# Attention and a mixture of experts in one kernel: the last two attention pairs in turn, and the late routing in two chains

## The chip, the cores and the metric

The kernel runs on one core of a Trainium2 chip. The metric is the time of one execution in microseconds (us) of device time. The core has five engines with a queue each: PE (matrix products; PEld is its weight load), DVE (vector), ACT (scalar), POOL, and SP, which here only issues DMAs. Each engine takes its instructions in the order in which the program lists them; semaphores make one engine wait for another.

## What is computed

Queries, pooled in pairs of rows, attend to keys; the result is the input of a mixture of eight experts with the two best per token.

```python
B, H, S, D = q.shape                      # 4, 8, 1152, 64
q_pool = q.reshape(B, H, S // 2, 2, D).mean(axis=3)
scores = scale * np.matmul(q_pool, k.transpose(0, 1, 3, 2))
attn = softmax(scores)                    # minus the row's maximum, over the sum
x = np.matmul(attn, v)                    # -> (2304, 512): 4 x 576 tokens, 8 heads x 64
noisy = x @ w_gate + np.log1p(np.exp(x @ w_noise)) * noise
top2, top2_w = the two best of 8 experts, softmax over the two
for e in range(8):                        # w1: 512 x 1024, w2: 1024 x 512
    out[mask] += top2_w * (np.maximum(x[mask] @ w1[e], 0) @ w2[e])
```

## The kernel before

**Attention.** A pair is one head of two batches: sixteen pairs, i = 0 to 15, eight (one per head) for the first half of the tokens and eight for the second. A pair has nine chunks of 128 queries; three chunks are a segment, so there are 48 segments, n = 0 to 47, and segment n belongs to pair n // 3 and query group g = n % 3. Numbers are split into a high and a low 16-bit part, so that each product is made of several. Ahead of a pair's segments stands its preparation: loads (load_k, load_q, load_v: kr, qr, vr), high and low parts (kn, qn, vv), DMA transpositions (kt, qt), a copy of the keys (kt2), the maximum of the scores of each query (products on PE, L297, and reductions on DVE), and the transposition of the maxima with the queries' low part (qt2). A segment is worked in nine steps of 128 keys; two steps make a unit u, 216 units in all. Of a unit, PE makes the scores (L342, L343), ACT the exponential pf (L350), DVE or POOL the low part pl (L354), and PE, some four units later, the products with the values (L370, P x V below). When a segment is through, it is evacuated (L381 to L390) into xa (first half) or xr (second half), one tile per query group.

**The planner.** The attention phase and what is laid among it is not issued in the order of the code. Plan collects operations, each with its engine, an estimated cost, a key (its due time, in steps of 128 keys), the operations that it depends on and the buffers that it takes and gives back, and then issues, engine by engine, the one with the lowest key of those that can start within 0.25 us of the earliest. So keys, costs and dependences set the order on every engine; once issued, an engine's order is fixed. Keys of a pair's preparation are counted from b = 27 * i.

**Routing.** Route.steps(j, gs, ...) routes the query groups gs of half j: three DMA transpositions per group (xTg, L661), 36 small products (L671), a chain of small DVE instructions (tiles rt and ru, L675 to L789), in it a product that ranks the tokens (the rank product, L757 and L759), and at its end six scatters per group, which POOL issues as indirect DMAs and which write the tokens into each expert's list xg in DRAM (L99). The first half is one chain of three groups, laid among attention by the planner with a pace between the keys of its steps. The second half is three chains, one per group, each of which starts when that group's segments of all eight pairs are evacuated. They are soft: what is not issued when attention is through goes on as a generator between the blocks of the early experts (Moe.early).

**Experts.** The first 256 rows of the lists of experts 0 and 1 come from the first half alone. Route.early loads them by DMA transpositions (xe, and the tokens' meta rows, mte); its operations become ready 20 us after the last scatter of the first half has been issued. Moe.early works experts 0 and 1 on them: eight blocks f of products (L927, mm1), each with a high part hh on ACT and a low part hl on DVE (L936, L937), and two blocks of 24 products (L948, mm2), while the next weights are split (wh on ACT, wl on DVE, L872 and L874). Then Moe.run loads the remaining rows (xT, L882), which needs every scatter, and works all eight experts in full; that is the full expert stage.

## Time and profile before

| | us |
|---|---|
| median of the three runs shown | 912.49 |
| lowest and highest of them | 906.23, 916.42 |
| span of the profiled execution | 910.5 |
| PE busy | 830.6 (91%) |
| DVE busy | 532.0 (58%) |
| ACT busy | 446.5 (49%) |
| POOL busy | 369.0 (41%) |
| chain that ended last: PE, DVE, DMA | 69%, 15%, 6% |

The span goes from the first to the last instruction of one execution taken by the profiler. Busy shares are means over stages with different limits, so a stage has to be looked at by itself. PEclk is the matrix engine's granted clock as a share of full speed. In a timeline a row is the start, the duration, the engine, the line and what is written from what; the brackets at its end say how long the engine stood idle before it, and what released it. A pipelined product's duration overlaps the next one's.

### The profile page before, as it was taken

To read this page: it belongs to the slowest core of one execution; us is meant where nothing else is said; L and a number is where in the kernel's file an instruction comes from. 1 tells how busy PE (TensorE), PEld (TensorE's weight loads), DVE (VectorE), ACT (ScalarE), POOL (GpSimd) and SP (SyncE) were. 2 spreads that over 40 slices of the span, in tenths; PEclk is the share of its full clock that TensorE was granted. 3 is DMA by queue.
4 is the path that set the end of the run, shared out by engine and by line. 5 is a ranking of instruction groups with operands and counts; after the bars stand their busy time and mean duration, and the time that the engine had idled before them with its cause. 6 is when DMAs were issued, how large, how long until landed. Compare 5 with 4: busy or idle time off the path is not lost.

```text
span 910.5 us, 21013 instructions
## 1 busy us (share of the span) xinstructions
PE 830.6 (91%) x8686; PEld 542.0 (60%) x8686; DVE 532.0 (58%) x1248; ACT 446.5 (49%) x663; POOL 369.0 (41%) x326
## 2 busy tenths in 40 slices
PE   3799899999999788899968899999999999999995
PEld 0367666667677666677754455657465565746542
DVE  4988887988897798898858233343324241431200
ACT  4678787777776556677523223333333232322310
POOL 4347577666765576777204611010211203020132
PEclk9889999999999899999988999999999999999998
DMA  8898976898697935475486956363736437281133
GB/s 192 198 242 165 209 208 177 178 215 191 142 225 163 201 94 127 125 206 170 106 131 224 298 71 163 71 183 97 205 74 169 110 111 184 77 208 24 24 49 46
DMA packets 213636, 137.79 MB, mean 151 GB/s; under 512 B 150304, under 2 KB 183584, under 8 KB 213536
## 3 DMA queue, kind: packets, MB, share of 16 engines
q1 hardware_dynamic: 204896, 116.33, 52.6%
q0 software_dynamic: 8640, 20.08, 10.7%
q8 instruction: 69, 1.13, 0.5%
q14 instruction: 31, 0.25, 0.1%
HBM read 62.14 MB, written 35.44 MB: 107 GB/s over the span
## 4 chain that ended last, share of the span: by engine, by line
PE 69%; DVE 15%; DMA 6%; issue 5%; ACT 2%; POOL 2%; SPq 1%; POOLq 0%; ACTq 0%; DVEq 0%
PE pss L927 21%; PE psm L948 20%; PE psm L370 11%; PE psm L297 6%; PE pss L342 5%; PE pss L343 5%; DVE pl L354 3%; DVE rd L311 2%; DMA vr<-in_v_dram 1%; POOL xg L99 1%; DVE vv L281 1%; DVE mx L320 1%; PE psm L927 1%; DMA kr<-in_k_dram 1%; ACT pf L350 1%
## 5 line engine op out<-in xcount | busy, mean ns | idle before, releaser
L354 POOL TENSOR_TENSOR pl<-pf 128x768 f16<-128x768 f32 x149 | 236.1, 1596 | 133.0 <-ACT pf L350 124.0
L350 ACT ACTIVATE pf<-pss 128x768 f32<-128x768 f32 x216 | 174.2, 811 | 75.6 <-PE pss L343 70.0
L99 POOL DMA_INDIRECT out_dram<-y,mti x40 | 62.6, 1565 | 323.4 <-ACT y L953 318.1
L370 PEld LDWEIGHTS <-pf 128*128 128x128 bf16 (+1 forms) x2880 | 156.2, 101 | 61.7 <-issue 21.5
L370 PE MATMUL psm<-vv,pf 128*128 128x65 f16 (+2 forms) x2880 | 189.0, 199 | 2.3 <-DVE vv L281 0.9
L370 PE MATMUL psm<-vv,pl 128*128 128x65 f16 (+1 forms) x1440 | 176.5, 194 | 0.2 <-DVE pl L354 0.2
L342 PE MATMUL pss<-qt,kt 128*128 128x384 f16 (+1 forms) x576 | 150.8, 290 | 1.8 <-ACT pf L350 1.6
L343 PE MATMUL pss<-qt,kt 66*128 66x384 f16 (+1 forms) x576 | 151.3, 291 | 0.0
L937 DVE SCALAR_TENSOR_TENSOR hl<-pss,hh 128x640 f16<-128x640 f32 (+2 forms) x68 | 50.2, 738 | 156.8 <-ACT hh L936 156.8
L370 PEld LDWEIGHTS <-pl 128*128 128x128 f16 (+1 forms) x1440 | 127.5, 103 | 1.3 <-issue 1.0
L948 PE MATMUL psm<-wh,hh 128*128 128x512 f16 x320 | 122.7, 383 | 3.6 <-issue 3.6
L948 PE MATMUL psm<-wl,hh 128*128 128x512 f16 x320 | 122.7, 383 | 0.0
L948 PE MATMUL psm<-wh,hl 128*128 128x512 f16 x320 | 122.3, 382 | 0.0
L948 PEld LDWEIGHTS <-hh 128*128 128x128 f16 x640 | 62.8, 98 | 79.0 <-issue 6.2
L311 DVE CUSTOM_DVE_ANT_0 rd<-psm,rd 128x512 f32<-128x512 f32 x144 | 97.1, 683 | 19.8 <-ACT rd L305 19.2
L936 ACT ACTIVATE hh<-pss 128x640 f16<-128x640 f32 (+2 forms) x68 | 43.2, 635 | 131.5 <-PE pss L927 131.4
L953 ACT ACTIVATE y<-psm,mg 128x512 f32<-128x512 f32 x40 | 27.5, 689 | 152.5 <-issue 77.3
L305 ACT ACTIVATE rd<-psm 128x512 f32<-128x512 f32 x144 | 85.7, 596 | 27.2 <-PE psm L297 17.3
L297 PE MATMUL psm<-kt,qt 128*128 128x512 f16 (+3 forms) x320 | 78.8, 323 | 20.9 <-ACT rd L305 10.0
L927 PE MATMUL pss<-xT,fh 128*128 128x320 f16 (+1 forms) x448 | 83.5, 303 | 1.1 <-DMA xT<-xg 1.1
L927 PE MATMUL pss<-xT,wh 128*128 128x320 f16 (+1 forms) x448 | 83.5, 303 | 0.0
L297 PE MATMUL psm<-kd,qt 128*128 128x512 f16 (+1 forms) x160 | 59.0, 412 | 26.6 <-DVE mx L311 14.6
(157 smaller groups left out, 1196.2 us busy)
## 6 DMA issues: line engine op xcount, KB each, us to landing
xg<-zt SPq DMA_DIRECT2D x40, 260.0 KB
kr<-in_k_dram SPq DMA_DIRECT2D x32, 288.0 KB
vr<-in_v_dram SPq DMA_DIRECT2D x16, 576.0 KB
kr<-in_moe_w_dram SPq DMA_DIRECT2D x17, 512.0 KB
qr<-in_moe_w_dram SPq DMA_DIRECT2D x16, 512.0 KB
kn<-in_moe_w_dram SPq DMA_DIRECT2D x16, 512.0 KB
qr<-in_q_dram SPq DMA_DIRECT2D x31, 256.0 KB
vr<-in_moe_w_dram SPq DMA_DIRECT2D x15, 512.0 KB
```

What stands on the lines that cost most here:

```text
L99: i = nc.gpsimd.indirect_dma_start(out=out, out_offset=bass.IndirectOffsetOnAxis(ap=idx, axis=0), in_=src, in_offset=None, **kw)
L297: s.nc.tensor.matmul(ps[r, o:o + m.shape[1] * P], s.G.buf["qt", i][:, c, r], m, start=True, stop=True)
L305: s.nc.scalar.activation(s.G.buf["rd", i, c], s.G.buf["D", i, c], AF.Relu)
L311: s.nc.vector.tensor_tensor_reduce(out=rd, in0=s.G.buf["S", i, c], in1=rd, scale=1.0, scalar=-3.0e38, op0=ALU.add, op1=ALU.max, accum_out= ...
L342: mm(ps[:, a, o:o + w], kt[:, hh * NK + kc, :], qf[:, q0:q0 + w], start=True, stop=False)
L343: mm(ps[:, a, o:o + w], kt2[0:66, hh * NK + kc, :], qf2[0:66, q0:q0 + w], start=False, stop=True)
L350: s.nc.scalar.activation(s.parts(u)[0], s.G.buf["ps", u][:, :, 0:SG], AF.Exp, scale=0.125 / (IN_SCALE * IN_SCALE))
L354: (s.nc.vector if eng == "DVE" else s.nc.gpsimd).tensor_sub(pl, pf, ph)
L370: mm(ps[o:o + m, ci, 0:w], src[:, t % 2, ci * P + o:ci * P + o + m], vv[:, hh * NK + kc, a:b], start=st, stop=last and src is pl, skip_gro ...
L927: nc.tensor.matmul(ps[:, i, 0:N], w[:, dc, f * P:(f + 1) * P], xT[:, 2 * dc + x, i * N:(i + 1) * N], start=(n == 0), stop=(n == 11))
L937: s.nc.vector.scalar_tensor_tensor(hl, ps, 0.0, hh, op0=ALU.max, op1=ALU.subtract)
L948: nc.tensor.matmul(ps, h[:, f, b * P:(b + 1) * P], w[:, f, :], start=(n == 0), stop=(n == 23))
```

## The change

Four things are changed.

The order of the last six segments: a table SEQ says which pair and group segment n belongs to. Up to pair 13 it is as before; pairs 14 and 15 take turns, (14, 0), (15, 0), (14, 1), (15, 1), (14, 2), (15, 2). The preparation of pairs from 10 on gets earlier keys, three less for each pair, and the last evacuation gets an earlier one.

The late routing: groups 0 and 1 of the second half are one chain (its tiles are of six chunks instead of three), whose second group's transpositions depend on that group's own evacuations (more); group 2 is a second chain. Their operations on other engines than DVE have keys lower by 12.

The first half's routing: its first key is 245 instead of 250, its pace 0.8 instead of 1.2, its scatters follow each other at 2.5 us instead of 3.0, and the early expert loads become ready 10 us after it instead of 20.

In Moe.early the meta instructions of an early expert come behind its eight blocks.

```diff
+SEQ = [(i, g) for i in range(NPAIR - 2) for g in range(3)] + [(i, g) for g in range(3) for i in (NPAIR - 2, NPAIR - 1)]
             n, kc = divmod(2 * u + a, NK)
-            i, g = divmod(n, 3)
+            i, g = SEQ[n]
...
-            b = 27 * i
+            b = 27 * i - 3 * max(0, i - 9)
...
-                           lat=3.0, take=[("qt2", ("qt2", i))] if g == 0 or not x else (), give=[("qn2", i)], after=ready[0][0] if x and g else None)
-                    for y in ((m,) if x else (m - 2, m - 1, m)):
-                        ready[y] = [t] + [kc[h] for h in ((0,), (0, 1), (1,))[y % 3]]
+                           lat=3.0, take=[("qt2", ("qt2", i))] if g == 0 or not x else (), give=[("qn2", i)], after=ready[0, 0][0] if x and g else None)
+                    for y in ((g,) if x else (0, 1, 2)):
+                        ready[i, y] = [t] + [kc[h] for h in ((0,), (0, 1), (1,))[y]]
+            b = 9 * SEQ.index((i, 0))
...
-            pr = sorted({n // 3 for n in segs})
-            sc = op("PE", 0.66, 2 * u, lambda u=u: s.score(u), deps=[d for n in segs for d in ready[n]], take=[("wide", ("ps", u))],
+            pr = sorted({SEQ[n][0] for n in segs})
+            sc = op("PE", 0.66, 2 * u, lambda u=u: s.score(u), deps=[d for n in segs for d in ready[SEQ[n]]], take=[("wide", ("ps", u))],
                     give=[(x, i) for i in pr for x in ("kt", "kt2", "qt", "qt2")])
...
-            i = n // 3
+            i, g = SEQ[n]
...
-            k1 = 9 * n + 17
+            k1 = 9 * n + (17 if n < NSEG - 1 else 7)
-            s.ev[n] = op("DVE", 0.3, k1 + 1, lambda n=n: s.evac(n, 2), deps=[hi], give=[("pv", n)])
+            s.ev[i, g] = op("DVE", 0.3, k1 + 1, lambda n=n: s.evac(n, 2), deps=[hi], give=[("pv", n)])
...
         def then():
             for e in range(NEARLY):
-                op("SP", 2.6, 400 + 4 * e, lambda e=e: R.early(e), ready=G.now + 20.0)
-        s.route(R.steps(0, (0, 1, 2), s.sm, 14, 6, 0.8), 250, [s.ev[n] for n in range(24)], 3.0, then=then, pace=1.2)
-        for g in range(3):
-            s.route(R.steps(1, (g,), R.rp, 36, 15, 0.3), 450 + 9 * g, [s.ev[24 + 3 * i + g] for i in range(NH)], 0.7, True)
-
-    def route(s, gen, key, deps, slack, soft=False, then=None, pace=0.0):
+                op("SP", 2.6, 400 + 4 * e, lambda e=e: R.early(e), ready=G.now + 10.0)
+        s.route(R.steps(0, (0, 1, 2), s.sm, 14, 6, 0.8), 245, [s.ev[i, g] for i in range(NH) for g in range(3)], 3.0, then=then, pace=0.8)
+        late = [[s.ev[i, g] for i in range(NH, NPAIR)] for g in range(3)]
+        s.route(R.steps(1, (0, 1), R.rp, 14, 6, 0.3), 432, late[0], 0.7, True, more=late[1])
+        s.route(R.steps(1, (2,), R.rp, 18, 8, 0.3), 450, late[2], 0.7, True)
...
+    def route(s, gen, key, deps, slack, soft=False, then=None, pace=0.0, more=()):
...
-            G.op(eng, cost, due[0], lambda: piece(bank, held), deps=deps, gen=gen if soft else None, **kw)
+            G.op(eng, cost, due[0] - (12 if soft and eng != "DVE" else 0), lambda: piece(bank, held), deps=deps, gen=gen if soft else None, **kw)
...
             wait, eng, cost = d if isinstance(d, tuple) else (0.0, "DVE", 0.3)
+            nxt = more if eng == "SP" and wait == 0.0 else ()
...
             else:
-                add(eng, cost, ready=ready)
+                add(eng, cost, ready=ready, deps=nxt)
...
-                yield (3.0 if j == 0 else 0.3, "POOL", 1.3) if gap else None
+                yield (2.5 if j == 0 else 0.3, "POOL", 1.3) if gap else None
...
                 yield 1.28
-                if f == 0:
-                    s.meta(e, 0, EARLY)
                 s.flush(KEEP)
                 for c in SPL[f]:
                     s.split(e, "2", c)
             s.flush()
+            s.meta(e, 0, EARLY)
```

The other two uses of divmod(n, 3), in pv and evac, are replaced like the first.

What this does to the order on the engines, in three places. The first is on SP, in the middle of the first half's routing (its groups' transpositions are xTg from xa). Before, the value load of pair 11 (vr) came behind the kt2 copies and a qt2 transposition:

```order
L661 DMA_TRANSPOSE xTg_5063<-xa2_133 128x8x128
L661 DMA_TRANSPOSE xTg_5085<-xa2_133 128x8x128
L661 DMA_TRANSPOSE xTg_5104<-xa2_133 128x8x128
L428 DMA kt2_0_121<-kt_0_94 64x1152 x2
L287 DMA_TRANSPOSE qt2_1_106<-qn2_1_127 128x9x128
L277 DMA vr_72<-in_v_dram 128x2x576
```

Now it stands ahead of them, with one clearing of the output between it and the transpositions:

```order
L665 DMA_TRANSPOSE xTg_4947<-xa2_133 128x8x128
L665 DMA_TRANSPOSE xTg_4968<-xa2_133 128x8x128
L665 DMA_TRANSPOSE xTg_4991<-xa2_133 128x8x128
L520 DMA out_0_dram<-zt_130 128x2x256
L278 DMA vr_72<-in_v_dram 128x2x576
L288 DMA_TRANSPOSE qt2_1_106<-qn2_1_127 128x9x128
L429 DMA kt2_0_121<-kt_0_94 64x1152
```

The second place is on SP at the end of attention. xr0 to xr2 are the second half's groups, L803 and L806 (now L807 and L810) loads of the first expert's weights, qt2_1_106 is the buffer of pair 15's maxima. Before, from pair 14's values on:

```order
L277 DMA vr_72<-in_v_dram 128x2x576 x2
L287 DMA_TRANSPOSE qt2_1_106<-qn2_1_127 128x9x128
L803 DMA kr_70<-in_moe_w1_dram 128x1024
L806 DMA qr_71<-in_moe_w2_dram 128x2x512
L806 DMA kn_73<-in_moe_w2_dram 128x2x512
L806 DMA vr_72<-in_moe_w2_dram 128x2x512
L806 DMA kr_70<-in_moe_w2_dram 128x2x512
L661 DMA_TRANSPOSE xTg_7818<-xr0_83 128x8x128
L661 DMA_TRANSPOSE xTg_7850<-xr0_83 128x8x128
L661 DMA_TRANSPOSE xTg_7882<-xr0_83 128x8x128
L661 DMA_TRANSPOSE xTg_7951<-xr1_84 128x8x128
L630 DMA_TRANSPOSE xe0_7971<-xg_82 128x8x256
```

Now, from the same load on (L288 is L287 of before, L634 and L636 are L630 and L632, L665 is L661):

```order
L278 DMA vr_72<-in_v_dram 128x2x576
L634 DMA_TRANSPOSE xe0_7058<-xg_82 128x8x256
L636 DMA mte0_7060<-xg_82 128x2x16
L634 DMA_TRANSPOSE xe1_7120<-xg_82 128x8x256
L636 DMA mte1_7122<-xg_82 128x2x16
L288 DMA_TRANSPOSE qt2_1_106<-qn2_1_127 128x9x128
L278 DMA vr_72<-in_v_dram 128x2x576
L807 DMA kr_70<-in_moe_w1_dram 128x1024
L810 DMA qr_71<-in_moe_w2_dram 128x2x512
L810 DMA vr_72<-in_moe_w2_dram 128x2x512
L810 DMA kn_73<-in_moe_w2_dram 128x2x512
L665 DMA_TRANSPOSE xTg_7587<-xr0_83 128x8x128
```

The early expert loads xe0 and xe1 with their meta rows moved from behind the late groups' first transpositions to ahead of pair 15's qt2; pair 15's values come behind that.

The third place is on PE in the first early expert. Before, the first rank product (tri and ones, for group 0 of the second half alone) stood six products into mm2:

```order
L948 LDWEIGHTS hl_8060
L948 MATMUL psm1_66<-wh2_8088,hl_8060 128x512
L757 LDWEIGHTS tri_353
L757 MATMUL psm2_67<-ru3_8362,tri_353 128x32
L759 LDWEIGHTS ones_355
L759 MATMUL psm2_67<-ru3_8362,ones_355 128x24
L759 LDWEIGHTS ones_355
L759 MATMUL psm2_67<-ru3_8362,ones_355 128x16
L759 LDWEIGHTS ones_355
L759 MATMUL psm2_67<-ru3_8362,ones_355 128x8
L948 LDWEIGHTS hh_8059
```

Now the rank product, of groups 0 and 1 together, stands behind the sixth block of mm1, f = 5, whose last products are the first rows here; the ones of the other chunks and then block f = 6 follow it:

```order
L931 MATMUL psm0_65<-xe0_7058,fh_86 128x256
L931 LDWEIGHTS fl_87
L931 MATMUL psm0_65<-xe0_7058,fl_87 128x256
L761 LDWEIGHTS tri_353
L761 MATMUL psm1_66<-ru6_8262,tri_353 128x56
L763 LDWEIGHTS ones_355
L763 MATMUL psm1_66<-ru6_8262,ones_355 128x48
L763 LDWEIGHTS ones_355
L763 MATMUL psm1_66<-ru6_8262,ones_355 128x40
L763 LDWEIGHTS ones_355
L763 MATMUL psm1_66<-ru6_8262,ones_355 128x32
L763 LDWEIGHTS ones_355
```

The rank product moved ahead of two blocks of mm1 and six products of mm2. The route products of groups 0 and 1 moved ahead of the last P x V product; before, group 0's stood right behind it and the others between the blocks of the first early expert. Group 2's stand behind block f = 6.

## Rows read from the trace of the kernel before

**Rows 1.** The view of the cores: span and mean granted clock.
```profile
core 0: 910.5 us, clock 0.971
```
**Rows 2.** Windows: length, busy (instructions) of PE, PEld, DVE, ACT, POOL; PEclk, DMA, GB/s.
```profile
290.00:400.00 110.00, 94.94 (x1430) 70.19 (x1427) 92.80 (x244) 67.94 (x106) 76.44 (x63) 0.94 0.64 152
...
497.00:525.00 28.00, 23.34 (x146) 14.35 (x145) 9.94 (x29) 8.68 (x15) 19.52 (x30) 0.94 0.93 287
525.00:895.00 370.00, 369.69 (x2188) 214.01 (x2188) 110.84 (x178) 110.90 (x147) 56.16 (x70) 1.00 0.48 113
```
**Rows 3.** Chain that ended last, from attention's end on: start, us, what.
```profile
452.58 3.01 PE psm L370 x93
...
456.39 5.16 DMA xe<-xg
461.59 2.72 PE pss L927 x12
...
470.08 1.31 PE psm L927 x12
471.39 0.89 PE psm L671 x36
...
513.56 4.70 DMA xg<-xr,rt
518.80 6.47 DMA xT<-xg
525.31 31.36 PE pss L927 x192
556.67 15.54 PE psm L948 x72
```
**Rows 4.** Timeline, DVE, first early expert and late routing.
```profile
462.19 0.17 DVE L894 TENSOR_SCALAR mq<-mte 128x4 f32<-128x4 f32 x1 [4.87 <-DMA mte<-xg]
...
462.88 1.23 DVE L874 SCALAR_TENSOR_TENSOR wl<-qr,wh 128x1024 f16<-128x1024 f32 x1
...
464.23 0.18 DVE L682 TENSOR_SCALAR rt<-rt 128x24 f32<-128x24 f32 x1
464.44 0.18 DVE L685 TENSOR_SCALAR rt<-rt 128x24 f32<-128x24 f32 x1
...
464.76 0.42 DVE L937 SCALAR_TENSOR_TENSOR hl<-pss,hh 128x256 f16<-128x256 f32 x1
```
**Rows 5.** Timeline, SP's queue and then ACT, around a value load.
```profile
300.86 1.44 SPq L428 DMA_DIRECT2D kt<-kt  x2
...
303.85 0.69 SPq L277 DMA_DIRECT2D vr<-in_v_dram  x1
...
310.42 1.18 ACT L284 ACTIVATE vv<-vr 128x1152 f16<-128x1152 f32 x1 [4.97 <-DMA vr<-in_v_dram]
```
**Rows 6.** Windows of the exponentials alone (x counts them).
```profile
375.00:400.00 25.00, 11.22 (x14) 1.00 0.65 186
```
**Rows 7.** Routing tiles at 293 to 366: count, then ns least/median/most, first and last start.
```profile
L720 DVE SCALAR_TENSOR_TENSOR rt<-rt,rt x6: 223/1143/1532, 326.5 to 335.8; 128x72 f32<-128x72 f32 x6
```
**Rows 8.** Timeline, PE, second early expert.
```profile
516.55 0.61 PE L948 MATMUL psm<-wh,hh 128*128 128x512 f16 x1 [3.04 <-issue]
```
**Rows 9.** Timeline, POOL, the last two scatters of the second half.
```profile
512.28 0.97 POOL L99 DMA_INDIRECT xg<-xr,rt  x1 [0.21 <-issue]
...
513.56 0.97 POOL L99 DMA_INDIRECT xg<-xr,rt  x1 [0.21 <-issue]
```
**Rows 10.** POOL by line at 362 to 432: count, busy us, mean ns, idle before it.
```profile
L354 POOL TENSOR_TENSOR pl<-pf 128x768 f16<-128x768 f32 x19 | 29.8, 1579 | 11.9 <-ACT pf L350 9.5 <-DVE pl L354 2.2
L99 POOL DMA_INDIRECT xg<-xa,rt x18 | 22.5, 1248 | 4.2 <-issue 2.9 <-DVE xa L789 1.2
```
**Rows 11.** Timeline, SP's queue, the early expert loads and what follows.
```profile
456.39 2.92 SPq L630 DMA_TRANSPOSE xe<-xg  x1
...
462.85 11.43 SPq L661 DMA_TRANSPOSE xTg<-xr  x5
```

More of the change, by code (lines that the diff above doesn't have):

```diff
@@ L357, in pv @@
         mm = s.nc.tensor.matmul
-        i, g = divmod(n, 3)
+        i, g = SEQ[n]
         t = n * NK + kc
@@ L374, in evac @@
         nc = s.nc
-        i, g = divmod(n, 3)
+        i, g = SEQ[n]
         j, h = divmod(i, NH)
@@ L496, in pairs @@
         for n in range(NSEG):
-            i = n // 3
+            i, g = SEQ[n]
             done = []
```

## The prediction

> **What bounds the kernel now.** I read the span first, then the windows of busy time by engine, then the chain that ended last, and only then the timelines of single engines in the stretches that the chain points at. The span of the profiled execution is 910.5 us [rows 1]; the median of the three runs shown is 912.49 us, so what is worked out against the span gets 2.0 us added at the end. The windows show three stages [rows 2]. From 525 on the matrix engine is busy 369.69 us of 370: nothing in the change touches that stage. Up to 455 is attention, with the first half's routing at 290 to 400, where the matrix engine is idle 110 - 94.94 = 15.1 us. Between them lies the handover, with the second half's routing and the two early experts. The chain [rows 3] shows its length: the last P x V products start at 452.58 and run 3.0 us, to about 455.5 (I use 455.4); the full expert stage starts at 525.31. That is 69.9 us. What is left after 525.31 is 910.5 - 525.3 = 385.2 us.
>
> The handover's own matrix work is small. Twelve 256-column products take 1.31 us at full clock and 72 products of 512 columns 15.54 us, so 24 take 5.18 us [rows 3]. One early expert is 8 x 1.31 + 2 x 5.18 = 20.8 us; two are 41.7 us. The other 28 us are waits and stretches at the lower of the clock's two levels: the first twelve products behind the 5.16 us wait for xe took 2.72 us instead of 1.31 [rows 3].
>
> **The change, part by part.** *The xe loads go earlier.* The sync engine's rows put them before the last pair's qt2 transposition, not behind the late groups' transpositions. If the first half's scatters have landed by then, the 5.16 us wait goes, and the lower clock behind it (2.72 - 1.31 = 1.4 us in the first block and about 0.4 in the second: 1.8). The vector engine's 4.87 us wait for the expert's meta rows [rows 4] goes too, since meta now stands behind the eight blocks.
>
> *Route products inside attention.* Thirty-six route products take 0.89 us [rows 3]. Those of groups 0 and 1 now stand before the last P x V product; group 0's used to run in the xe wait. The matrix engine is full there, so this costs 2 x 0.9 = 1.8 us.
>
> *The value load.* At 310.42 the scalar engine had waited 4.97 us for a value load, which the sync engine issued at 303.85, behind two kt copies and a qt2 transposition that began at 300.86 [rows 5]. In the new order that load stands ahead of these: 303.85 - 300.86 = 3.0 us earlier. I take 2.8 us off; the bounds are 0 (another load is late instead: the one before it now stands behind three xTg transpositions) and 5.0.
>
> *Two tight transfers.* Group 1's xTg transpositions must land within the last segment, and the last pair's qt2 waits for the pair before it to give its buffer back one segment ahead of use. The trace has neither; the nearest row is xe, 5.16 us from issue to use [rows 3], against four to four and a half exponential units of cover, 1.79 us each [rows 6]: 7 to 8 us. I take 1 us for both; bounds 0 and 2 x 5.16 = 10.3. So attention's end stays where it is: 455.4 + 1.8 - 2.8 + 1.0 = 455.4.
>
> *Pairs in turn, closer steps.* The same products, exponentials and routing instructions are issued; I take 0. Bounds: the 15.1 us of idle time at 290 to 400 [rows 2] is the most that a better order can return, and a loss can be as large: by the order, eight more exponential units than before (8 x 1.79 = 14 us [rows 6]) come behind the last max pass, where nothing is left to run beside them. One thing speaks against closer steps: six equal route instructions show 223 ns at best and 1143 ns at the median [rows 7], in a stretch where the pool engine is subtracting. The Trainium skill, page "SBUF — State Buffer", section "Who interferes with whom", says that a vector instruction with two SBUF inputs and a pool instruction that reads SBUF exclude each other, whoever starts first. The trace agrees with it in that the same instruction takes 0.22 us or over 1.1; by that rule closer steps would get no cheaper, since the pool engine's subtractions there are as many as before.
>
> *The handover, walked through.* Count from the last P x V product (t = 0). The vector engine has the chain of groups 0 and 1 as one of 48 elements, not two of 24. Of about 45 steps 12 run just before the last evacuation. Dependent steps follow each other every 0.21 us [rows 4]; I take 0.24 for twice the elements. Route evacuation at -1.5, twelve steps to +1.0, last evacuation and two steps to 2.7, waiting for the first high half to 3.3. Then four low halves of w2 at 1.15 and four hl at 0.35 (1.23 and 0.42 busy [rows 4], but the next instruction starts a little earlier) and about 33 steps, 6.3 us in all: 4.6 + 1.4 + 6.3, to 15.6. The matrix engine has done six blocks by 6 x 1.31 = 7.9 and stands at the rank product, whose operand is ready at 15.6: **7.7 us idle is what is late next**, and the lower clock doubles the next block, 2.6 us. Then 1.2 for group 2's route products, 1.3 waiting for hl, 1.3 for the last block, 5.2 and 2.6 of products: 29.8. Group 2's chain on the vector engine starts at 20 (its evacuation waits for the route products) and passes 45 steps (8.0 us), two hl, meta (0.7) and three low halves (3.5): rank operand ready at 33.0. Wait 3.2, rank and twelve products 2.8, lower clock 1.5 (a wait of 3.04 us was followed by a product of 0.61 us [rows 8], against 5.18 us for 24): the first expert ends at 37.5.
>
> The second expert is 20.8 us. Before, it filled the 28 us from 497 to 525 [rows 2], among them a wait of 3.04 us without a named releaser [rows 8]: 28 - 20.8, less the 1.1 us that xT came late, is 6 us over, with scatters in flight nearly all the time. Now they are for about a third of it. I take 2 of the 6 us; bounds 0 and 6. End: 60.3. The transfers are ready earlier: twelve scatters from 20.5 every 1.28 us [rows 9] to 36, six more to 44, the last starts at 42.7; 4.70 to land, 0.5, and 6.47 for xT [rows 3] make 54.4. So the matrix engine sets the end, and the saving in scatters alone is worth nothing beyond that.
>
> **Sum.** 455.4 + 60.3 + 385.2 = 900.9 us of span against 910.5: 9.6 less. With 2.0 added, 903 us, 1.0% under the median. About 1% is also what a measurement of this kernel can tell from no change.
>
> **Rivals.** *A: less comes back.* The second expert keeps its 6 us and the value load's stall only moves (2.8): 903 + 4 + 2.8 = 910. For it: the waits of the second expert are not named by a releaser that the change removes.
> *B: only the xe wait goes.* The merged chain is still too late for the rank product, waits as long as two chains did, and the change does not do what it says: 903 + 9.6 - 5.2 = 907. Against it: 33 steps of one chain are left, where two had 90.
> *C: attention gains.* Half of the 15.1 us idle at 290 to 400 comes back: 895. For it: the routing ends some nine exponential units earlier; against: the vector engine is busy 92.80 of those 110 us [rows 2] and does the same work.
> *D, the other side: the sync queue blocks on xe.* xe waits for all eighteen scatters; behind it in the queue stand the last pair's qt2 and values. Eighteen scatters took 22.5 us with 4.2 us of idle time ahead of them, and the subtractions 1.58 us each [rows 10]. In the new order about 14 subtractions stand between them: 27 + 22 = 49 us of pool work, across 23 exponential units of 1.79 us [rows 6], 41 us: up to 8 us late. The four xe transfers hold the queue 462.85 - 456.39 = 6.5 us [rows 11]. By my count xe starts some 1 us before it would delay qt2; from there each us costs one. It decides when the scatters are more than 10 us late, which eats the 9.6. Were each of these 32 pool steps a third longer, 65 us, they would be 24 late: 903 + 23 = 926; halfway to it, 919, is what I put down for this case.
>
> **How the numbers follow.** My forecast, 903, has 0.45; its own range is 897 to 909 (attention's bounds, the second expert's 0 to 6). A 0.18, B 0.10, C 0.16, D 0.11. Faster by over 1% means under 903.4: half of the forecast (0.24), C, and a little of the rest: 0.43. Slower, over 921.6, is part of D and what I do not see: 0.11. Within 1%: 0.46. The range goes from C's 895, a little lower, to 914: it leaves out most of D and the strong end of C.
>
> **What would show it.** In the profile after: no wait for xe, the first expert block right behind the last P x V product; the matrix engine's longest wait of the handover at the rank product of groups 0 and 1, 6 to 9 us; the full expert stage from about 516; the wait at 305 to 312 smaller; the last qt2 issued without a wait behind xe. I am wrong if attention ends more than 5 us from 455, if the sync queue stands at xe, or if the rank product comes without a wait.

## The result and the profile after

The changed kernel is slower: 919.33 us against 911.59 us, medians of ten runs each, ratio 1.0075 with the interval 1.0049 to 1.0101. Executions more than 1.5% above the fastest of the same kernel are left out of all medians and ratios here. The forecast was 903 with a range to 914. The stages of one profiled execution of each say where it went:

| us, profiled execution | before | forecast | after |
|---|---|---|---|
| end of the last P x V product | 455.6 | 455.4 | 474.8 |
| start of the full expert stage | 525.3 | 515.7 | 532.3 |
| handover between them | 69.7 | 60.3 | 57.5 |
| from there to the end | 385.2 | 385.2 | 385.5 |

The handover gave back 12 us, a little more than forecast. Attention, forecast as unchanged, took 19 us more.

Not all of the 19 us come from the change. Up to 223 us both programs issue the same instructions in the same order on every engine. The exponentials of units 96 and 135 (units counted from 0), in the kernel before and then in the changed one:

```profile
220.76 0.81 ACT L350 ACTIVATE pf<-pss 128x768 f32<-128x768 f32 x1
...
297.76 0.79 ACT L350 ACTIVATE pf<-pss 128x768 f32<-128x768 f32 x1
```

```profile
222.35 0.80 ACT L351 ACTIVATE pf<-pss 128x768 f32<-128x768 f32 x1
...
305.56 0.81 ACT L351 ACTIVATE pf<-pss 128x768 f32<-128x768 f32 x1
```

At unit 96 the changed kernel is 1.6 us late, which is the spread between two executions. From unit 96 to unit 135 it takes 83.2 us instead of 77.0 (6.2 more), and from there to attention's end 169.2 instead of 157.8 (11.4 more). These 17.6 us are what has to be explained.

Windows of busy time of the changed kernel; columns as in [rows 2], the third column from the end is the granted clock:

```profile
0.00:474.65 474.65, 416.62 (x6143) 300.56 (x6144) 382.67 (x857) 313.98 (x479) 280.11 (x208) 0.94 0.76 173
...
290.00:400.00 110.00, 93.06 (x1288) 66.84 (x1286) 87.22 (x237) 64.26 (x98) 72.38 (x65) 0.84 0.71 171
```

The same of the kernel before, attention only:

```profile
0.00:455.60 455.60, 403.92 (x6077) 292.66 (x6078) 381.79 (x848) 313.81 (x479) 282.48 (x209) 0.97 0.76 177
```

The vector, scalar and pool engines are busy as long as before, to 2.4 us. The matrix engine is busy 416.62 - 403.92 = 12.7 us longer and idle 58.0 instead of 51.7 us, 6.3 more. Of the 12.7, the 72 route products that moved in are 1.8 (two times 0.9); the other 10.9 us are the same products at the lower clock (mean 0.94, was 0.97). At 290 to 400 the clock is 0.84, where it was 0.94 [rows 2].

The matrix engine's waits, timeline of the changed kernel (the first two in attention, the others in the handover):

```profile
284.73 0.33 PE L298 MATMUL psm<-kt,qt 128*128 128x128 f16 x3 [4.48 <-DVE mx L312]
...
322.31 0.59 PE L298 MATMUL psm<-kd,qt 128*128 128x512 f16 x1 [5.72 <-DVE mx L312]
...
474.63 0.38 PE L931 MATMUL pss<-xe,fh 128*128 128x256 f16 x2
...
489.98 0.20 PE L761 MATMUL psm<-ru,tri 128*128 128x56 f16 x1 [5.77 <-DVE ru L758]
...
506.51 0.18 PE L761 MATMUL psm<-ru,tri 128*128 128x32 f16 x1 [2.40 <-DVE ru L758]
...
532.27 0.48 PE L931 MATMUL pss<-xT,fh 128*128 128x384 f16 x2 [0.38 <-DMA xT<-xg]
```

Two waits of 4.48 and 5.72 us for a max reduction (mx, written at L312) are new. The kernel before had, between 215 and 440, no such wait over 2.14 us, and one of 4.23 us for the scalar engine:

```profile
274.72 0.38 PE L297 MATMUL psm<-kd,qt 128*128 128x512 f16 x1 [2.14 <-DVE mx L311]
...
312.12 0.64 PE L297 MATMUL psm<-kt,qt 128*64 128x512 f16 x2 [4.23 <-ACT rd L305]
```

What the vector engine did ahead of the second wait, and the pool engine beside it:

```profile
312.73 7.51 DVE L704 SCALAR_TENSOR_TENSOR rt<-rt,rt 128x72 f32<-128x72 f32 x6
```

```profile
311.17 8.71 POOL L355 TENSOR_TENSOR pl<-pf 128x768 f16<-128x768 f32 x6 [1.32 <-ACT pf L351]
```

Six equal routing steps take 7.51 us together. The last of them, when the pool engine had nothing left, took 0.23; the five ahead of it 7.25, that is 1.45 each, which is 8.71 / 6, one subtraction. Step and subtraction alternate. In the vector engine's order nineteen routing rows stand in a row here (twelve before), and the max reduction for which the matrix engine waits is behind them.

The first wait has the same look. Three vector instructions stand in a row ahead of the reduction (L312), and each has a subtraction beside it:

```profile
277.64 2.34 DVE L282 SCALAR_TENSOR_TENSOR vv<-vr,vv 128x1152 f16<-128x1152 f32 x1
279.91 2.02 DVE L282 SCALAR_TENSOR_TENSOR kn<-kr,kn 128x576 f16<-128x576 f32 x1
281.85 2.22 DVE L355 TENSOR_TENSOR pl<-pf 128x768 f16<-128x768 f32 x1
283.99 0.68 DVE L312 CUSTOM_DVE_ANT_0 rd<-psm,rd 128x512 f32<-128x512 f32 x1
```

```profile
277.31 1.47 POOL L355 TENSOR_TENSOR pl<-pf 128x768 f16<-128x768 f32 x1 [2.03 <-ACT pf L351]
279.85 3.40 POOL L355 TENSOR_TENSOR pl<-pf 128x768 f16<-128x768 f32 x2 [1.08 <-ACT pf L351]
```

Further on in the trace the same kinds take 1.35, 0.75 and 0.95 us.

### The profile page after: what moved, and what is told of

Read it like the earlier page. It is cut to its first block, busy times and chain, and to the rows that moved or that the text cites. A ratio compares the mean times of both kernels' runs of the same rounds, so it can differ in the third digit from the quotient of the medians.

```text
span 917.8 us, 20943 instructions
## 1 busy us (share of the span) xinstructions
PE 837.6 (91%) x8685; PEld 547.0 (60%) x8685; DVE 531.5 (58%) x1205; ACT 445.8 (49%) x662; POOL 366.8 (40%) x325
## 3 DMA queue, kind: packets, MB, share of 16 engines
q0 software_dynamic: 8640, 20.08, 10.9%
## 4 chain that ended last, share of the span: by engine, by line
PE 71%; DVE 16%; DMA 4%; issue 4%; ACT 2%; POOL 2%; SPq 0%; POOLq 0%; ACTq 0%; DVEq 0%
PE pss L931 20%; PE psm L952 20%; PE psm L371 13%; PE psm L298 6%; PE pss L343 5%; PE pss L344 5%; DVE pl L355 3%; DVE rd L312 3%; POOL xg L100 1%; DVE vv L282 1%; DMA xg<-zt 1%; DVE rt L704 1%; ACT pf L351 1%; DMA kr<-in_k_dram 1%; DVE kn L282 1%
## 5 line engine op out<-in xcount | busy, mean ns | idle before, releaser
L371 PEld LDWEIGHTS <-pf 128*128 128x128 bf16 (+1 forms) x2880 | 160.0, 102 | 60.3 <-issue 19.6
L371 PE MATMUL psm<-vv,pf 128*128 128x65 f16 (+2 forms) x2880 | 193.8, 201 | 1.9 <-DVE vv L282 1.2
L371 PE MATMUL psm<-vv,pl 128*128 128x65 f16 (+1 forms) x1440 | 180.2, 197 | 3.1 <-DVE pl L355 3.1
L343 PE MATMUL pss<-qt,kt 128*128 128x384 f16 (+1 forms) x576 | 153.9, 295 | 2.4 <-ACT pf L351 2.4
L344 PE MATMUL pss<-qt,kt 66*128 66x384 f16 (+1 forms) x576 | 154.4, 296 | 0.0
L371 PEld LDWEIGHTS <-pl 128*128 128x128 f16 (+1 forms) x1440 | 129.7, 105 | 4.7 <-DVE pl L355 3.2
L312 DVE CUSTOM_DVE_ANT_0 rd<-psm,rd 128x512 f32<-128x512 f32 x144 | 97.4, 684 | 30.1 <-ACT rd L306 29.1
L298 PE MATMUL psm<-kd,qt 128*128 128x512 f16 (+1 forms) x160 | 60.3, 421 | 28.2 <-DVE mx L312 16.1
```

Of the source, the lines that this page charges most:

```text
L298: s.nc.tensor.matmul(ps[r, o:o + m.shape[1] * P], s.G.buf["qt", i][:, c, r], m, start=True, stop=True)
L312: s.nc.vector.tensor_tensor_reduce(out=rd, in0=s.G.buf["S", i, c], in1=rd, scale=1.0, scalar=-3.0e38, op0=ALU.add, op1=ALU.max, accum_out= ...
L343: mm(ps[:, a, o:o + w], kt[:, hh * NK + kc, :], qf[:, q0:q0 + w], start=True, stop=False)
L344: mm(ps[:, a, o:o + w], kt2[0:66, hh * NK + kc, :], qf2[0:66, q0:q0 + w], start=False, stop=True)
L371: mm(ps[o:o + m, ci, 0:w], src[:, t % 2, ci * P + o:ci * P + o + m], vv[:, hh * NK + kc, a:b], start=st, stop=last and src is pl, skip_gro ...
```

## The experiments

Attention's end and the handover are read from one profiled execution each; attention whose order is that of before ended at 455.6 in one and at 449.8 in another (e4), so differences under 6 us of such a single end are not read. Counted from the exponential of unit 96 on, up to which the order is the same in all kernels here, the two differ by 3.9 us (234.8 and 230.9). Ratios are to the kernel before, run beside it.

**Which of the changes (e1 to e4).** Each part of the change undone or alone:

```
e1: 245 -> 250, pace=0.8 -> 1.2, 2.5 -> 3.0, G.now + 10.0 -> G.now + 20.0     (in after)
e2: the same four numbers the other way, and nothing else                     (in before)
e3: SEQ, b = 27 * i - 3 * max(0, i - 9), last evacuation's key                (in before)
e4: steps(1, (0, 1), ...) and steps(1, (2,), ...), keys - 12, meta moved      (in before)
```

> The changed kernel with the first half's routing as it was before (first key 250, pace 1.2, scatters every 3.0 us, early expert loads ready 20 us after it); pairs in turn and the merged late routing stay. Theory 1, the closer steps of the first half's routing block the vector engine and cost the 19 us of attention: attention ends at 455 to 460 instead of 474.6, total 903 to 907 (the handover may get up to 5 us longer, as the xe loads come later). Theory 2, the pairs in turn with their earlier preparation cost them: attention ends at 470 to 476, total 917 to 922. If both have a share, it ends between, and the other kernels of this set say how much.

> The kernel before with only the first half's routing changed (first key 245, pace 0.8, scatters every 2.5 us, loads ready after 10 us). Theory 1: attention ends at 468 to 475 instead of 455.4, less up to 5.2 us for the xe wait that goes: total 919 to 926. Theory 2: attention ends at 453 to 458 and the xe wait goes: total 906 to 912.

> The kernel before with only the order of the last six segments, the earlier keys of the preparation from pair 10 on and the earlier last evacuation. Theory 1: attention ends at 454 to 459, total 911 to 916. Theory 2: attention ends at 468 to 475, and the handover, whose late routing has the groups a segment apart, stays near 65 to 70 us: total 920 to 931.

> The kernel before with only the late routing changed (groups 0 and 1 one chain, lower keys off the vector engine, the expert's meta behind its eight blocks). Both theories: attention unchanged within 2 us (455.4). The handover was 69.9 us before and 57.6 us in the changed kernel; here the xe wait of 5.2 us and its clock (1.8 us) stay, so 62 to 67 us: total 904 to 909.

| | attention ends | from unit 96 on | handover | total | ratio |
|---|---|---|---|---|---|
| before | 455.6 | 234.8 | 69.7 | | |
| changed | 474.8 | 252.4 | 57.5 | 919.3 | 1.0075 (1.0049 to 1.0101) |
| e1, all but the first half | 457.5 | 237.7 | 58.4 | 907.1 | 0.9951 (0.9923 to 0.9979) |
| e2, the first half alone | 457.0 | 236.1 | 58.2 | 904.6 | 0.9922 (0.9897 to 0.9947) |
| e3, pairs in turn alone | 456.0 | 232.9 | 69.0 | 916.8 | 1.0059 (1.0015 to 1.0102) |
| e4, late routing alone | 449.8 | 230.9 | 79.3 | 920.9 | 1.0125 (1.0072 to 1.0179) |

Both theories fell. In these traces neither the closer steps alone nor the pairs in turn alone lengthen attention; only together do they: 455.6 with neither, 456.0 to 457.5 with one, 474.8 with both. One thing stays open: e3's total is 0.6% longer than before, and its trace does not show where, for the profiled execution (914.3) is 2.6 us under the median of its kernel. The gain of the handover comes in either way: the first half's settings alone give 58.2, the pairs in turn with the late routing 58.4, all of it 57.5. It is one gain, not two.

e4 missed too, the other way. The merged chain without pairs in turn makes the handover 10 us longer. From the matrix engine's timeline of e4:

```profile
452.96 0.38 PE L931 MATMUL pss<-xe,fh 128*128 128x256 f16 x2 [1.98 <-DMA xe<-xg]
...
484.64 0.19 PE L761 MATMUL psm<-ru,tri 128*128 128x32 f16 x1 [3.60 <-DVE ru L758]
...
529.17 0.80 PE L931 MATMUL pss<-xT,fh 128*128 128x384 f16 x2 [18.71 <-DMA xT<-xg]
```

The first rank operand is there 35 us after attention's end (in the changed kernel 15), and the full stage waits 18.71 us for its tokens. Without turns groups 0 and 1 end two segments and one segment before attention does, with turns four and two.

**Does the pool engine set the price (e5, e6, e9, e10).** The order on all engines stays that of the changed kernel; only the subtractions get shorter, half of the low parts left out:

```diff
+        if eng == "POOL" and 118 <= u < 165:      # e9: 118 <= u < 130, e10: 136 <= u < 152
+            pl, pf, ph = pl[:, 0:1], pf[:, 0:1], ph[:, 0:1]
```

e6 is the same edit in e1's kernel.

> The changed kernel with the same order on every engine, but the pool engine's subtractions of the low parts of units 118 to 164 do only half of their columns (the other half of these low parts is left out). Theory 3, the vector engine's routing and splitting steps with two operands each wait for a running pool subtraction (five equal steps took 7.25 us beside six subtractions of 1.45 us), so that the max reductions behind them come late: the same five steps take 3.5 to 4.5 us, the wait of 5.72 us of the matrix engine behind them is under 3.5, and attention ends at 458 to 467 instead of 474.8. Rival, the order alone (max reductions stand behind nineteen routing rows, whatever these last): the wait stays over 4.5 us and attention ends at 470 to 475.

> The same halving of the pool subtractions of units 118 to 164 (half of these low parts left out) in the kernel with the first half's routing as before and everything else changed, whose attention ended at 457.5. Theory 3: it gains much less than the changed kernel does, 0 to 4 us, so it ends at 453 to 457.5. Rival, the subtractions cost as much in any order: it gains as much as the changed kernel does.

> The changed kernel, same order, pool subtractions halved (half of these low parts left out) for units 118 to 129 only, which lie beside the three long vector steps ahead of the 4.48 us wait at 284.7. If these steps are long because they wait for the pool engine: that wait falls under 2.5 us, the 5.72 us wait behind the routing run stays over 4.5, the granted clock at 325 to 350 stays under 0.85, attention ends at 465 to 471 instead of 474.8. If the subtractions do not matter there: the 4.48 us wait stays and attention ends at 473 to 476.

> The changed kernel, same order, pool subtractions halved (half of these low parts left out) for units 136 to 151 only, beside the run of nineteen routing rows. If the run is long because each of its steps waits for a subtraction: the five equal steps take 3.5 to 4.5 us instead of 7.25, the 5.72 us wait falls under 3.5, the granted clock behind it (325 to 350) rises from 0.70 to over 0.85, the wait of 4.48 us ahead of it stays, and attention ends at 461 to 468. If not: the 5.72 us wait stays and attention ends at 473 to 476.

Attention ended at 452.0 in e5, at 443.2 in e6, at 466.1 in e9 and at 455.8 in e10. Part of these differences stands ahead of the edits (3.4 us in e10, 3.0 in e9, spread as above), so the stretches say more:

| us | unit 96 to 135 | from there to attention's end | handover |
|---|---|---|---|
| before | 77.0 | 157.8 | 69.7 |
| changed | 83.2 | 169.2 | 57.5 |
| e5, units 118 to 164 halved | 78.0 | 150.3 | 61.6 |
| e9, units 118 to 129 halved | 79.5 | 167.3 | 58.8 |
| e10, units 136 to 151 halved | 83.2 | 153.6 | 57.6 |
| e1 | 76.9 | 160.8 | 58.4 |
| e6, e1 with units 118 to 164 halved | 75.3 | 146.1 | 61.8 |

Up to the place of its edit e10 repeats the changed kernel to 0.1 us. e9 gets back 3.7 us around the first wait, e10 gets back 15.6 behind unit 135, while the first wait stays. e9 came as expected; e5 and e10 ended attention earlier than either of their two cases. e10's vector engine, and its matrix engine:

```profile
307.39 2.60 DVE L706 SCALAR_TENSOR_TENSOR rt<-rt,rt 128x72 f32<-128x72 f32 x6
```

```profile
281.33 0.33 PE L298 MATMUL psm<-kt,qt 128*128 128x128 f16 x3 [4.48 <-DVE mx L312]
```

The six steps take 2.60 us instead of 7.51: only two of them still meet a subtraction and take 0.75 each, the others 0.23. The wait of 5.72 us has no row any more. Its clock, and that of the changed kernel in the same window:

```profile
325.00:350.00 25.00, 20.22 (x264) 13.46 (x262) 22.87 (x79) 16.04 (x27) 14.87 (x20) 0.93 0.73 179
```

```profile
325.00:350.00 25.00, 22.73 (x262) 15.41 (x261) 15.27 (x64) 12.46 (x21) 13.44 (x10) 0.70 0.36 90
```

In e6, theory 3 expected 0 to 4 us and it gained 16 over e1 in the two stretches: shorter subtractions help any order of this kernel. e5 gained 24 over the changed kernel, so the part that belongs to the changed order is some 8 us, a difference of four single attentions. For the same reason e10's 15.6 are more than the 11.4 that were lost behind unit 135. So these kernels show that the pool engine's work beside the run carries the loss, not yet whether by the length of the single subtraction or by the amount of work, since half of the work was gone too.

**Length or amount (e13, with e14 and e15 in two faster kernels).** All of the work, in pieces of half the length:

```diff
+        if eng == "POOL" and 136 <= u < 152:      # e14, e15: 130 <= u < 156
+            for h in range(2):
+                s.nc.gpsimd.tensor_sub(pl[:, h:h + 1], pf[:, h:h + 1], ph[:, h:h + 1])
+            return
```

> The changed kernel, everything computed, with each pool subtraction of units 136 to 151 issued as two of half the columns. If the price of a routing step is one running pool instruction, whatever its length: the five equal steps take 4 to 5 us instead of 7.25, the wait of 5.72 us behind them is under 4, attention ends at 457 to 466 instead of 474.8, total 902 to 911. If it is the amount of pool work beside them, which stays the same: the steps take 6.5 to 7.5 us, the wait stays over 5, total 916 to 921.

> The kernel before with the first half's routing changed and the pool subtractions of units 130 to 155 each issued as two halves. The one without halves stood 4.73 us at 311 behind the routing run and ended attention at 457.0, total 904.6. If halves shorten the run: that wait is under 3 us, attention ends at 450 to 455, total 898 to 903. If the pool's second issue costs what the steps gain: 904 to 908.

> The changed kernel with the preparation's keys earlier only from pair 13 on, and the pool subtractions of units 130 to 155 each issued as two halves. Without halves: a wait of 4.73 us at 312, attention to 456.5, total 905.2. If halves shorten the run: the wait is under 3 us, attention ends at 449 to 454, total 897 to 902. If not: 904 to 908.

e13: 915.4 us, ratio 0.9986 (0.9959 to 1.0013), attention to 469.5, handover 61.5. From unit 96 to 135 it takes 83.3 us, from there to attention's end 162.0. The steps came out as the first expectation has them; attention and total lie between the two. Its vector, pool and matrix engines at the run:

```profile
313.28 4.69 DVE L708 SCALAR_TENSOR_TENSOR rt<-rt,rt 128x72 f32<-128x72 f32 x6
```

```profile
313.13 9.53 POOL L357 TENSOR_TENSOR pl<-pf 128x384 f16<-128x384 f32 x12 [1.18 <-ACT pf L351]
```

```profile
321.07 0.58 PE L298 MATMUL psm<-kd,qt 128*128 128x512 f16 x1 [2.52 <-DVE mx L312]
323.68 0.59 PE L298 MATMUL psm<-kt,qt 128*128 128x512 f16 x1 [2.03 <-DVE mx L312]
```

4.69 / 6 = 0.78 us a step, and 9.53 / 12 = 0.79 us a piece: a step costs one running pool instruction, at both lengths that were run. The Trainium skill, page "SBUF — State Buffer", section "Summary: rules for kernel authors", says that when a vector instruction has two SBUF inputs while the pool engine's instruction reads SBUF, the second one to issue blocks until the first finishes; these two rates agree with it. So the length of the single subtraction, with all of the work done, carries 169.2 - 162.0 = 7.2 of the 11.4 us; by the ratios it is 1.0075 - 0.9986 = 0.9%, about 8 us.

The wait itself gave little of it: 5.72 us became 2.52 and 2.03, 1.2 less together. The rest is the clock. e13's windows behind the run:

```profile
320.00:325.00 5.00, 1.90 (x14) 1.13 (x14) 4.79 (x16) 0.60 (x1) 2.66 (x4) 0.60 0.00 0
325.00:330.00 5.00, 5.00 (x64) 3.79 (x63) 1.78 (x7) 1.62 (x2) 2.36 (x3) 0.72 0.71 159
330.00:335.00 5.00, 5.00 (x85) 3.59 (x84) 4.90 (x18) 3.24 (x6) 4.55 (x7) 1.00 0.29 105
```

The lower level lasts some 7 us here and 20 in the changed kernel (its windows stand further down). By these windows I estimate that the products there lost some 2 us to it in e13, 8 in the changed kernel and nothing in e10. With the waits that makes 7 us for e13 and 14 for e10, where 7.2 and 15.6 were measured: what e10 got back beyond e13 is mostly the rest of the wait and of the lower clock. In the faster kernels splitting gave nothing that stands out: e14 905.2 (0.9891, 0.9831 to 0.9952), e15 906.3 (0.9882, 0.9820 to 0.9945), where the wait behind the run fell only from 4.73 to 3.97 us.

**What collides (e7, e8, e17).** The first half's key and pace back (e7), or the earlier preparation of pairs 10 to 12 back (e8), or both (e17), with the rest of the change left in (pairs 13 and 14 get later keys too, by 6 and 3 steps):

```diff
-            b = 27 * i - 3 * max(0, i - 9)
+            b = 27 * i - 6 * max(0, i - 12)       # e8, e17
```
```
e7, e17: first key 245 -> 250, pace=0.8 -> 1.2
```

> The changed kernel with the first half's first key and pace as before (250, 1.2); scatters every 2.5 us and loads ready after 10 us stay. Theory, key and pace do the damage: attention ends at 455 to 460, the handover is 57 to 60 us, total 903 to 908. Rival, the closer scatters and the early loads on the pool and sync queues do it: attention ends at 468 to 475, total 913 to 920.

> The changed kernel with the preparation's keys earlier only from pair 13 on (six less for each pair, the same 18 at pair 15), so that pairs 10 to 12, which are prepared beside the first half's routing, have the keys of before. Theory, the earlier preparation and the closer routing collide on the vector engine: attention ends at 455 to 461, total 902 to 909. Rival, it is the pairs in turn or the routing alone: attention ends at 468 to 475, total 914 to 920.

> The changed kernel with the preparation's keys earlier only from pair 13 on, and the first half's first key and pace as before (scatters every 2.5 us, loads ready after 10 us). Neither half of the collision is left: no run of more than twelve routing rows ahead of a max reduction, attention ends at 450 to 456, handover 57 to 61 us, total 896 to 904. If the two cost the same as one: attention 456 to 459, total 904 to 908.

e7: 906.0 us, 0.9927 (0.9890 to 0.9964; its profiled execution, 916.4, is far from that, so its stages aren't read). e8: 905.2, 0.9926 (0.9896 to 0.9955), attention to 456.5, handover 60.4. e17: 906.4, 0.9927 (0.9896 to 0.9958), attention to 460.0, handover 58.0, its second case. Taking back either side of the collision takes back the loss, and taking back both brings nothing more. In e17 the wait for a value load is back with the old pace, 5.72 us on the scalar engine and 4.98 on the matrix engine behind it, and may hide a gain. So it is the preparation of pairs 10 to 12, 3 to 9 steps earlier, laid over a first half's routing in closer steps.

e8 also shows what is not explained. It has the same run of nineteen routing rows, and so has e2, with the same wait of 4.73 us behind it:

```profile
304.71 5.08 DVE L704 SCALAR_TENSOR_TENSOR rt<-rt,rt 128x72 f32<-128x72 f32 x6
```

```profile
303.15 5.74 POOL L355 TENSOR_TENSOR pl<-pf 128x768 f16<-128x768 f32 x4 [1.34 <-DVE rt L696]
```

```profile
311.85 0.58 PE L298 MATMUL psm<-kt,qt 128*128 128x512 f16 x1 [4.73 <-DVE mx L312]
```

Four subtractions lay beside it, not six, so the steps took 5.08; but the wait of 4.73 us is nearly as long. What differs is what follows. Windows of 5 us, first of e8, then of the changed kernel:

```profile
310.00:315.00 5.00, 2.17 (x28) 1.57 (x28) 4.79 (x16) 0.83 (x2) 0.00 (x0) 0.50 0.08 10
315.00:320.00 5.00, 5.00 (x74) 4.57 (x72) 4.86 (x11) 2.20 (x4) 3.40 (x2) 0.62 0.56 155
320.00:325.00 5.00, 4.92 (x75) 3.07 (x74) 4.93 (x20) 3.77 (x6) 4.04 (x3) 1.00 0.25 71
```

```profile
320.00:325.00 5.00, 1.75 (x13) 0.98 (x13) 4.68 (x19) 0.60 (x1) 0.00 (x0) 0.50 0.00 0
325.00:330.00 5.00, 5.00 (x52) 3.68 (x50) 1.15 (x4) 1.62 (x2) 1.77 (x2) 0.50 0.67 148
330.00:335.00 5.00, 5.00 (x50) 3.08 (x49) 3.67 (x11) 1.09 (x3) 2.64 (x2) 0.50 0.31 116
335.00:340.00 5.00, 5.00 (x54) 3.16 (x54) 2.88 (x30) 2.73 (x4) 3.37 (x3) 0.51 0.00 0
340.00:345.00 5.00, 5.00 (x82) 3.68 (x81) 3.44 (x7) 3.72 (x6) 3.65 (x3) 1.00 0.15 33
```

e8 is back at the full clock some 7 us behind the end of its wait at 311.85. The changed kernel stays at the lower of the two levels to about 340, more than 17 us behind the end of its wait at 322.31, fifteen of them with the matrix engine busy 5.00 of 5: at half the clock, some 8 us of products lost in one place (half of 1.75 + 15). Why the clock stayed low there is open. The wait of 4.48 us ahead of it is not the reason. In e9 only 1.92 us of that wait are left, the wait of 5.72 us, untouched, ends at 315.59, and the clock stays low for 14 us more:

```profile
315.59 0.58 PE L298 MATMUL psm<-kd,qt 128*128 128x512 f16 x1 [5.72 <-DVE mx L312]
```

```profile
325.00:330.00 5.00, 5.00 (x56) 3.26 (x54) 2.63 (x8) 1.84 (x3) 2.36 (x2) 0.50 0.01 2
330.00:335.00 5.00, 5.00 (x79) 3.52 (x77) 3.81 (x31) 4.11 (x8) 4.14 (x4) 1.00 0.15 33
```

**The handover (e11, e12, e16).** e8's kernel with the late routing in three chains (e11); e8's kernel with the late rank products later (e12); the kernel before with only the scatters' 2.5 us and the 10 us of the early loads (e16).

```
e11: for g in range(3): route(steps(1, (g,), ...), 450 + 9 * g, late[g], ...)
e12: yield (0.1 if j == 0 else 4.0, "PE", 0.6)          before the rank product
e16: 3.0 -> 2.5, G.now + 20.0 -> G.now + 10.0           (in before)
```

> The changed kernel with the preparation's keys earlier only from pair 13 on, and the late routing in three chains as before (the expert's meta stays behind its blocks). The one with the merged chain ended attention at 456.5 and took 60.4 us for the handover, of which 12.2 us were two waits for rank operands. If the merge is what shortens the handover: 65 to 70 us here, total 910 to 915. If the early xe loads alone do it, as in the first half's routing alone (58.2 us): 56 to 61 us, total 901 to 906.

> The changed kernel with the preparation's keys earlier only from pair 13 on, and the rank products of the second half 4 us later in the matrix engine's order (behind the eighth block of the first early expert and six products). If the two waits for rank operands (7.34 and 4.89 us) are a loss that other products could fill: they fall under 3 us together, the handover is 53 to 57 us instead of 60.4, total 898 to 902. Rival, the scatters then end too late and the wait moves to the full experts' token loads: handover 59 to 63 us, total 904 to 908.

> The kernel before with only the scatters of the first half every 2.5 us and the early expert loads ready after 10 us; its routing keeps its first key and pace, so its attention's order up to the scatters is that of before. If the early loads alone give the handover its gain: no wait for xe over 1 us, handover 56 to 62 us instead of 69.7, attention ends at 452 to 457, total 900 to 906. If the closer routing is needed for it: xe is still waited for, handover 66 to 70 us, total 909 to 913.

e11: handover 61.1, total 906.1 (0.9936, 0.9916 to 0.9957): with the early loads in place the merge is worth nothing that shows. e16: handover 62.2, total 908.4 (0.9959, 0.9925 to 0.9993), both a little above its first case: most of the handover's gain is the early loads, with the routing's pace untouched. e12: handover 58.2, total 906.9 (0.9951, 0.9931 to 0.9971). e8 waited 7.34 and 4.89 us for its rank operands; in e12 the matrix engine has no such wait over 0.3 us, and stands here instead:

```profile
515.27 0.80 PE L931 MATMUL pss<-xT,fh 128*128 128x384 f16 x2 [7.19 <-DMA xT<-xg]
```

The wait moved to the token loads. Some 58 us is the length of the other chain, routing, scatters and transfers; no kernel here has a shorter handover than 57.5.

## Why the prediction was wrong, step by step

**The step that failed** is "Pairs in turn, closer steps. The same products, exponentials and routing instructions are issued; I take 0." It measured some 16 us: the 17.6 from unit 96 on, less 1.8 for the route products, priced by themselves. In its place the runs showed that vector steps with two operands wait for a running pool subtraction (1.45 us each instead of 0.23), that two max reductions behind such steps come late, so that the matrix engine waits 4.48 and 5.72 us, and that its clock stays low behind the second wait. The sign of being wrong that the prediction had named, attention ending more than 5 us from 455, came true. The bound that stood beside it, a loss "as large" as 15.1 us, was the right order, but no rival was made of it, and the range ended at 914. Three things were in reach. The order of the changed program has nineteen routing rows in a row where there were twelve (e2 and e8 have them too, beside four subtractions instead of six and without the loss, so the count alone does not decide). [rows 7] showed the price of such a row beside pool work, 1143 ns at the median. And the rule that two-operand steps and pool reads exclude each other was named, with the conclusion that closer steps would "get no cheaper"; the question to ask was what stands behind a run of them: a max reduction on which the matrix engine waits.

**The term for the lower clock** was missing in attention. The 19 us, that spread included, are 1.8 of route products, 6.3 of idle time and 10.9 of the same products at a lower clock; I had counted the clock behind waits in the handover only.

**The value load.** Right as far as it goes: the scalar engine has no wait for a load left between 270 and 410. The 2.8 us did not come out at the end, since the longer waits took its place.

**Two tight transfers.** Right. Group 1's transposition took 3.92 us and the matrix engine waited 0.34 for it. From the chain that ended last of the changed kernel:

```profile
468.69 3.92 DMA xTg<-xr
472.65 0.47 PE psm L675 x12
...
519.54 6.59 DMA xg<-xr,rt
526.41 5.82 DMA xT<-xg
532.27 31.36 PE pss L931 x192
```

**Rival D**, the sync queue behind xe, did not happen. The last scatter of the first half was issued at 412.82, and on SP:

```profile
417.64 4.25 SPq L634 DMA_TRANSPOSE xe<-xg  x1
...
429.81 1.29 SPq L288 DMA_TRANSPOSE qt<-qn  x1
```

The last qt2 left 5 us after the last meta load, and no product waited for it. The eighteen scatters took 59 us, longer than the 49 counted, but attention was late by more than that. So the slower side came by another mechanism than the one I had put there, and that 919, written down for this case, is the measured time is chance. A, B and C did not happen either.

**The handover** was right in its walk. xe without a wait, the rank product 15.2 us after attention's end (forecast 15.6) with 5.77 us of waiting (7.7), the second one at 31.7 (33.0) with 2.40 (3.2), 57.5 in all (60.3). The 15.6 owes something to luck: about 33 steps were put at 6.3 us, 0.19 each, where 0.24 had been taken, which would make 7.9 and 17.2. One thing in the walk was wrong: the transfers were put at 54.4, six us of slack, and the matrix engine at the end of the chain. The last scatter was issued where forecast (45 us after attention's end, forecast 43), but took 6.59 us to land instead of 4.70 [rows 3], and the chain that ended last goes through it; the matrix engine waited 0.38 us for xT. e12, where the matrix engine waits 7.19 us for xT, says the same: there is no slack.

## What to carry to other kernels

On an engine that works in order, the price of a run of short steps is paid by what stands behind it: count, in the order of the changed program, the longest run ahead of an instruction on which the bounding engine waits, and price each step as it costs beside its neighbour (here one running pool instruction, not 0.23 us). The length of the run alone does not tell: e2 and e8 have the same nineteen rows beside four subtractions instead of six, and no loss. A planner that prices such a step at 0.3 us doesn't see this, so two edits that each leave attention as it was can collide; run them alone and together before adding up their gains. And when a change gives several reasons for one gain, look for the second chain that ends at the same time: here three ways led to the same 58 us.

None of the thirteen kernels that do all of the work is clearly faster than the smallest edit, the first half's routing alone (e2, 0.9922). e14 and e15 have the lowest ratios (0.9891 and 0.9882), but four executions each and intervals that hold e2's; e7, e8, e11 and e17 are level with it within theirs.

## What was not expected of the hardware

A vector step of 128 x 72 elements takes 0.23 us alone, 1.45 beside pool subtractions of 1.45 us, 0.78 beside pieces of 0.79: it waits out one whole pool instruction and the two engines take turns, so a small step costs what its neighbour costs. The granted clock stayed at 0.50 for more than 17 us behind a wait of 5.72 us (14 in e9), fifteen of them with the matrix engine busy 5.00 of 5 in every row, and for 7 us behind one of 4.73; what makes the difference was not found.
